# Four double blocks of layer one in teams, with pieces of plain items between the first team periods

## The chip, the cores and the metric

The kernel runs on one core of one Trainium2 chip. The metric is the time of one execution in microseconds on the device, as a median of several runs. TensorE does the matmuls, VectorE (DVE), ScalarE (ACT) and GpSimd (POOL) the elementwise work, and SyncE (SP) issues most of the transfers.

## What is computed

An attention over channels (256 x 256 scores over 6016 tokens) gives x, and two gated layers follow, each from 256 to 1536 and back to 256 features:

```
x1 = rmsnorm(x) * rms_g
y  = (silu(x1 @ w_gate) * (x1 @ w_val)) @ w_out          # layer one
z  = (sigmoid(y @ w2_gate) * (y @ w2_val)) @ w2_out      # layer two
```

## The kernel before

Every float32 operand is split into a high and a low part of the type that TensorE reads fast, and each product is three matmuls (`mm3`: high x high, high x low, low x high). The 6016 tokens are 47 tiles of 128, in 12 blocks of four tiles (block 5 has three). Two blocks are a pair, also called a double block; there are six, and pair 2, with block 5, is 448 columns wide per half, the others 512. The hidden features are 12 tiles, f = 0 to 11.

Layer one's first two pairs (blocks 0 to 3) are worked **plain**: an item is one block and one f. It has 12 matmuls for gate and value (`plain_gv`, into PSUM banks `g` and `v`) and 6 for the output, issued two items later (`SKEW`). Behind them ScalarE takes the gate, VectorE the product (L478), ScalarE the high part `hh` (L479) and VectorE the low part `hl` (L480). While the 48 plain items run, the weights of both layers are converted from 64-bit inputs in five groups of steps for each of 24 weight tiles (`conversion`, `ORDER`). `quota` says how many groups each item takes along, so that all are done five items ahead of the stage's end (`end`), and each tile of layer one before block 0 needs it (`ahead` lists which of the blocks 0 and 1 comes next).

All later pairs use a Strassen-like scheme with seven input products instead of eight (`product`: 11, S1, T2, 12, T3, S4, P4). One f of a pair is a **period**. Z, A and B are its PSUM accumulators. ScalarE copies Z to A (cpA), to `g1` (cpG) and to the bank for the fourth product (cpD), and B to `e5`; VectorE forms `v1` and `g1`; in the next period (`pv`) the gate is applied (gate, h1, h0) and the fourth product P4 is made.

Pair 2 of layer one is worked **alone** (`period`): it reads the plain stage's weights `wh`, `wl` in SBUF, and its output products are plain, four a period. All pairs after it are worked in **teams** (`joint`, `team_period`): six periods' hidden tiles `hs` are combined by a second seven-product scheme for the output, whose 21 products (`out_product`) run in the six periods that follow. Team periods read their split weights from DRAM (`gw_load` from `gd`, two periods ahead, three buffers) and combined output weights from `od` (`ow_load`). The six first team periods have no team before them to finish. Their order is the list NONE; later ones use EVEN and ODD.

Output weights reach `od` in halves: raw ones are read back (`out_load`), split (`out_high` on ScalarE, `out_low` on VectorE, which then stores), then combined on GpSimd (`out_sums`) and split again. Layer one's twelve halves and six of layer two's stand in the alone stage, the other six in layer one's later team periods. The alone stage also stores the gate and value weights into `gd` (`store_w`). The next pair is loaded and summed on GpSimd (`pair_load`, `pair_sums`) and split (`pair_high`, `pair_low`) during the current one. The order on every engine is that of the program; each engine works through its queue in order.

## Time and profile before

| | us |
|---|---|
| median of 3 runs | 1170.33 (1166.58 to 1170.48) |
| profiled execution | 1170.04 |
| its span, first to last instruction | 1168.3 |
| mean granted TensorE clock | 0.996 of full speed |

The attention takes the first 105 us; plain items follow to about 305, the alone stage to about 392, the first six team periods to about 424, and layer two's pairs begin near 660. In the rows below a line such as L480 is a line of the kernel before; PE is TensorE's matmuls, PEld its weight loads, and "x284" counts instructions that touch the stretch.

### The profile page before, as it was taken

The page shows a single profiled execution, that of the slowest core. Times are in us where ns is not written, and L with a number is a line of the kernel's source. Part 1 is how long each engine was busy: PE and PEld are TensorE (multiplying, and loading weights), DVE is VectorE, ACT ScalarE, POOL GpSimd, SP SyncE. Part 2 cuts the span into 40 slices and gives each one's busy share as a digit, 9 for nine tenths or more (in the row PEclk, how much of TensorE's full clock was granted, in tenths as well). Part 3 has the DMA queues.
Part 4 walks back from the last instruction along what each step waited for, and adds up shares of the span by engine and source line. Part 5 has one row for each costly group of instructions (what it writes and reads, how often), then busy time and mean ns, then how long its engine had stood idle before and what let it go on. Part 6 is the DMA issues. An engine that isn't in the chain of part 4 may idle for free.

```text
span 1168.3 us, 16678 instructions
## 1 busy us (share of the span) xinstructions
PE 1148.7 (98%) x5236; PEld 957.0 (82%) x5236; DVE 968.3 (83%) x1496; ACT 890.2 (76%) x1664; POOL 334.3 (29%) x398
## 2 busy tenths in 40 slices
PE   8899999999999999999999999999999999999998
PEld 7788788888898778888888788888888888888896
DVE  6798999886667688888888887888888888888877
ACT  6666788775577687887787887787787787787685
POOL 0043677454223322321321321311311321321121
PEclk9899999999999999999999999999999999999999
DMA  9663445867489989999999998998998998998995
GB/s 329 241 220 143 145 148 190 282 228 238 145 280 322 355 258 266 303 264 266 303 262 272 300 258 251 287 265 245 288 265 240 293 260 247 293 261 245 284 273 147
DMA packets 142856, 296.84 MB, mean 254 GB/s; under 512 B 13872, under 2 KB 53168, under 8 KB 142768
## 3 DMA queue, kind: packets, MB, share of 16 engines
q1 hardware_dynamic: 122032, 258.65, 65.6%
q0 software_dynamic: 20592, 37.00, 18.1%
q8 instruction: 41, 0.67, 0.2%
q14 instruction: 47, 0.39, 0.1%
q10 hardware_dynamic: 144, 0.13, 0.0%
HBM read 201.98 MB, written 56.75 MB: 221 GB/s over the span
## 4 chain that ended last, share of the span: by engine, by line
PE 84%; DVE 8%; DMA 4%; issue 2%; ACT 2%; POOL 1%; SPq 0%; DVEq 0%; POOLq 0%; ACTq 0%
PE g L107 12%; PE g L109 12%; PE g L108 12%; PE v L107 6%; PE v L108 6%; PE v L109 6%; PE y L108 5%; PE y L109 5%; PE y L107 5%; PE at L108 4%; PE at L107 4%; PE at L109 4%; DMA in<-in_q_dram 1%; PE y L973 1%; DVE xn L329 1%
## 5 line engine op out<-in xcount | busy, mean ns | idle before, releaser
L605 POOL DMA_DIRECT2D hs<-hs x143 | 124.7, 918 | 571.5 <-DVE hl L688 413.6
L688 DVE TENSOR_TENSOR hl<-hs,hh 128x512 fp32r<-128x512 f32 (+1 forms) x319 | 221.1, 704 | 25.1 <-ACT hh L657 24.2
L657 ACT CAST hh<-hs 128x512 fp32r<-128x512 f32 (+1 forms) x319 | 192.6, 615 | 25.7 <-PE at L109 6.5
L874 ACT COPY v<-g 128x512 f32<-128x512 f32 (+1 forms) x210 | 119.0, 567 | 63.1 <-PE g L109 59.8
L879 DVE TENSOR_TENSOR hs<-g,e 128x512 f32<-128x512 f32 (+1 forms) x105 | 71.5, 681 | 66.5 <-ACT v L874 65.6
L107 PE MATMUL g<-xh,gw 128*128 128x512 f32 x240 | 94.1, 392 | 0.7 <-DVE hs L879 0.6
L108 PE MATMUL g<-xl,gw 128*128 128x512 f32 x240 | 93.5, 389 | 0.0
L109 PE MATMUL g<-xh,gw 128*128 128x512 f32 x240 | 93.4, 389 | 0.0
L908 ACT ACTIVATE g<-g 128x512 f32<-128x512 f32 (+1 forms) x108 | 67.5, 625 | 30.4 <-DVE g L912 29.4
L107 PE MATMUL y<-hh,ow 128*128 128x512 f32 (+1 forms) x211 | 81.7, 387 | 0.2 <-issue 0.2
L108 PE MATMUL y<-hl,ow 128*128 128x512 f32 (+1 forms) x211 | 81.7, 387 | 0.0
L109 PE MATMUL y<-hh,ow 128*128 128x512 f32 (+1 forms) x211 | 81.6, 387 | 0.0
L874 ACT COPY g<-g 128x512 f32<-128x512 f32 (+1 forms) x105 | 61.3, 583 | 26.2 <-PE g L109 25.8
L912 DVE TENSOR_TENSOR g<-g,g 128x512 f32<-128x512 f32 (+1 forms) x105 | 70.3, 669 | 5.7 <-PE g L109 5.7
L883 ACT ACTIVATE sg<-v 128x512 f32<-128x512 f32 (+1 forms) x108 | 64.2, 594 | 7.5
L107 PE MATMUL g<-qh,gw 128*128 128x512 f32 (+1 forms) x171 | 66.5, 389 | 0.7 <-DVE hs L879 0.6
L109 PE MATMUL g<-qh,gw 128*128 128x512 f32 (+1 forms) x171 | 65.8, 385 | 0.0
L108 PE MATMUL g<-ql,gw 128*128 128x512 f32 (+1 forms) x171 | 65.8, 385 | 0.0
L108 PE MATMUL at<-hl,ow 128*128 128x512 f32 (+1 forms) x160 | 62.4, 390 | 0.6 <-DVE hl L688 0.6
L107 PE MATMUL at<-hh,ow 128*128 128x512 f32 (+1 forms) x160 | 62.2, 389 | 0.3 <-ACT hh L657 0.2
L109 PE MATMUL at<-hh,ow 128*128 128x512 f32 (+1 forms) x160 | 61.9, 387 | 0.0
L874 ACT COPY e<-g 128x512 f32<-128x512 f32 (+1 forms) x105 | 61.3, 584 | 0.4
(256 smaller groups left out, 3312.4 us busy)
## 6 DMA issues: line engine op xcount, KB each, us to landing
gw<-gd SPq DMA_DIRECT2D x216, 448.0 KB, 5.6
ow<-od SPq DMA_DIRECT2D x126, 384.0 KB, 5.4
hs<-hs POOLq DMA_DIRECT2D x128, 256.0 KB, 7.7
wraw<-in_w_dram SPq DMA_DIRECT2D x24, 768.0 KB, 5.3
od<-o SPq DMA_DIRECT2D x48, 256.0 KB, 4.6
vraw<-in_v_t_dram SPq DMA_DIRECT2D x11, 512.0 KB, 4.9
gd<-w2h SPq DMA_DIRECT2D x12, 448.0 KB, 2.6
gd<-w2l SPq DMA_DIRECT2D x12, 448.0 KB, 3.6
```

The lines of the kernel that those rows point to most:

```text
L107: nc.tensor.matmul(ps, sh, mh, start=start, stop=False, skip_group_check=more)
L108: nc.tensor.matmul(ps, sh, ml, start=False, stop=False, skip_group_check=more)
L109: nc.tensor.matmul(ps, sl, mh, start=False, stop=stop, skip_group_check=more)
L329: nc.vector.tensor_scalar_mul(xn[b][:, i], ps[i // 2][:, i % 2], rs[:, i : i + 1])
L605: nc.gpsimd.dma_start(out=to, in_=t, accum_op=ALU.add)
L657: nc.scalar.copy(h, src)
L688: nc.vector.tensor_sub(lo, src, f32(h))
L874: nc.scalar.copy(new(name, make, *args), s[src])
L879: nc.vector.tensor_add(s["v1"], s["Z"], s["e5"])
L883: nc.scalar.activation(out=new("sg0", lambda: t), in_=s["A"], func=acts[l])
L908: "gate": lambda: nc.scalar.activation(out=pv["g1"], in_=pv["g1"], func=acts[pl]),
L912: "g1": lambda: nc.vector.tensor_add(s["g1"], s["g1"], s["B"]),
```

## The change

- Pair 2 of layer one joins the teams, as layer one's last pair. `period` and `parts`, which worked it alone, are gone (not shown).
- The plain stage stops three items early (`LATE`). The pieces of these items (gate and value matmuls singly, output matmuls) go through the queue `plain` and take the two places "out" of the six first team periods. NONE has a new order, and Z and B of these periods stand in the single banks `y1` and `y0`.
- Layer one's split weights are stored to `gd` during the plain stage (`stored`, `store_plain`). The output weights in plain form go to `od` straight from `wh`, `wl` (`store_out`), so that of layer one only the combined halves are split, at hooks in the plain stage. Layer two's twelve halves are all split in the first six team periods (`soon_halves`).
- `ahead` puts block 0's items 8 and 9 one place later, and conversions must end at item 40 instead of 43.

```diff
...
+    LATE = 3
...
+    NW = NQ - A11
...
         def high():
             if l:
-                h = cv2.tile([P, NG, P], F32R, tag="w2h", name="w2h")
+                h = w["sh"] = cv2.tile([P, NG, P], F32R, tag="w2h", name="w2h")
+                nc.scalar.copy(h[:, A11:], w["t"][:, A11:NG])
             else:
-                h = wp.tile([P, NQ, P], F32R, tag=f"wh{f}", name="wh")
-            own = slice(A11, NG if l else NQ)
-            nc.scalar.copy(h[:, own], w["t"][:, own])
-            w["h"] = wh[l, f] = h
+                h = wh[l, f] = wp.tile([P, NW, P], F32R, tag=f"wh{f}", name="wh")
+                nc.scalar.copy(h, w["t"][:, A11:])
+            w["h"] = h
...
         def sums_high():
-            h = w["h"]
+            if not l:
+                w["sh"] = cv2.tile([P, NG, P], F32R, tag="w2h", name="w2h")
+            h = w["sh"]
             nc.scalar.copy(h[:, :A11], w["t"][:, :A11])
-            if l:
-                w["3h"] = h[:, S3 : S3 + 1]
-            else:
-                w["3h"] = cv1.tile([P, 1, P], F32R, tag="s3h", name="s3h")
-            nc.scalar.copy(w["3h"], w["s3"])
+            nc.scalar.copy(h[:, S3 : S3 + 1], w["s3"])
...
         def stored():
-            if l:
-                nc.sync.dma_start(out=gd[l][f][:, 0], in_=f32(w["h"]))
-                nc.sync.dma_start(out=gd[l][f][:, 1], in_=f32(w["l"]))
-                del wh[l, f], wl[l, f]
-            else:
-                nc.sync.dma_start(out=s3d[f][:, 0], in_=f32(w["3h"])[:, 0])
-                nc.sync.dma_start(out=s3d[f][:, 1], in_=f32(w["3l"])[:, 0])
+            for e, t in enumerate((w["sh"], w["sl"])):
+                if l:
+                    nc.sync.dma_start(out=gd[l][f][:, e], in_=f32(t))
+                else:
+                    nc.sync.dma_start(out=gd[l][f][:, e, :A11], in_=f32(t[:, :A11]))
+                    nc.sync.dma_start(out=gd[l][f][:, e, S3], in_=f32(t[:, S3]))
...
     ORDER = (
-        "-high units shifted", "-low", "whole signed", "size -s_high -s_low rounded", "guarded sums -stored"
+        "-high units shifted",
+        "-low",
+        "whole signed",
+        "size -s_high rounded -s_low -stored",
+        "guarded sums",
...
-    def plain_gv(it):
+    def plain_one(it, m, late=False):
         b, f = it
         w = sizes[b] * P
-        gv[it] = [gv_bank("g"), gv_bank("v")]
-        for m, ps in enumerate(gv[it]):
-            for c, (h, lo) in enumerate(xT[b]):
-                j = A11 + 2 * m + c
-                mm3(ps[:, :w], wh[0, f][:, j], wl[0, f][:, j], h[:, :w], lo[:, :w], c == 0, c == KC - 1)
+        ps = gv_bank("gv"[m and not late])
+        gv.setdefault(it, []).append(ps)
+        for c, (h, lo) in enumerate(xT[b]):
+            j = 2 * m + c
+            mm3(ps[:, :w], wh[0, f][:, j], wl[0, f][:, j], h[:, :w], lo[:, :w], c == 0, c == KC - 1)
+
+    def plain_gv(it):
+        plain_one(it, 0)
+        plain_one(it, 1)
...
-    alone = [(0, PLAIN, f) for f in range(NF)]
-    joint = [(0, p, f) for p in range(PLAIN + 1, NP) for f in range(NF)]
+    joint = [(0, p, f) for p in (*range(PLAIN + 1, NP), PLAIN) for f in range(NF)]
     joint += [(1, p, f) for p in (0, 1, 3, 4, 5, 2) for f in range(NF)]
-    stream = alone + joint
...
+    soon_pairs = [(1, i) for i in range(NF // 2)]
...
     def out_load(l, i):
-        if l and i < NJ:
-            w = [wp.tile([P, 2, 512], F32, tag=lent_out[(NJ * i + u) % 4], name="o") for u in range(3)]
-            o = [w[u // 2][:, u % 2] for u in range(5)]
+        if l == 0:
+            odd[l, i] = [cv2.tile([P, 512], F32, tag="ot", name="o")]
         else:
-            if l:
-                o = [ip3.tile([P, 512], F32, tag="yo", name="o") for _ in range(3)]
-            else:
-                o = [wp.tile([P, 512], F32, tag=lent_in[i], name="o") if i in lent_in else sp.tile([P, 512], F32, tag="t1", name="o")]
-                o += [sp.tile([P, 512], F32, tag=f"t{u}", name="o") for u in (2, 3)]
-            o += o[1:]
-        odd[l, i] = {"t": o[0], 0: o[1:3], 4: o[3:]}
-        nc.sync.dma_start(out=o[0], in_=rd[l][i].rearrange("p u n -> p (u n)"))
+            odd[l, i] = [sp.tile([P, 512], F32, tag=f"o{u}", name="o") for u in (i % 2, 2, 3)]
+        nc.sync.dma_start(out=odd[l, i][0], in_=rd[l][i].rearrange("p u n -> p (u n)"))
 
     def out_high(l, i, first):
-        nc.scalar.copy(odd[l, i][first][0].bitcast(F32R), odd[l, i]["t"])
+        if l == 0:
+            odd[l, i] += [cv2.tile([P, 512], F32, tag=t, name=t) for t in ("oh", "ol")]
+        elif first:
+            odd[l, i] = [odd[l, i][3]] + [sp.tile([P, 512], F32, tag=f"o{u}", name="o") for u in (4, 5)]
+        nc.scalar.copy(odd[l, i][1].bitcast(F32R), odd[l, i][0])
 
     def out_low(l, i, first):
-        h, lo = odd[l, i][first]
-        nc.vector.tensor_sub(lo.bitcast(F32R), odd[l, i]["t"], h)
+        h, lo = odd[l, i][1:3]
+        nc.vector.tensor_sub(lo.bitcast(F32R), odd[l, i][0], h)
         g, j = divmod(i, NJ)
         for e, t in enumerate((h, lo)):
             dst = od[l][g][:, first : first + 4, e, j]
             nc.sync.dma_start(out=dst, in_=t.rearrange("p (u n) -> p u n", u=4))
 
     def out_sums(l, i):
-        w11, w21, w12, w22 = (odd[l, i]["t"][:, u * P : (u + 1) * P] for u in range(4))
-        nc.gpsimd.tensor_add(w22, w21, w22)
-        nc.gpsimd.tensor_sub(w21, w11, w21)
-        nc.gpsimd.tensor_sub(w11, w22, w11)
-        nc.gpsimd.tensor_sub(w12, w11, w12)
+        o = odd[l, i]
+        if l:
+            o.append(sp.tile([P, 512], F32, tag=f"o{6 + i % 2}", name="o"))
+        w11, w21, w12, w22 = (o[0][:, u * P : (u + 1) * P] for u in range(4))
+        s2, s3, s4, s1 = (o[-1][:, u * P : (u + 1) * P] for u in range(4))
+        nc.gpsimd.tensor_add(s1, w21, w22)
+        nc.gpsimd.tensor_sub(s3, w11, w21)
+        nc.gpsimd.tensor_sub(s2, s1, w11)
+        nc.gpsimd.tensor_sub(s4, s2, w12)
...
     NONE = (
-        "11 S1 cpA gate h1 P4 third part1 T2 e5 12 flush h0 first"
-        " gw early part0 out out cpG ACT out sg T3 cpD out S4 end"
-        " DVE g1 v1"
+        "gate h1 11 gw P4 S1 h0 DVE cpA early T2 12 third e5"
+        " first cpG end T3 sg S4 cpD v1 ACT flush g1 out out"
...
         def out():
-            if outs:
-                outs.popleft()()
-                outs.popleft()()
+            if plain:
+                plain.popleft()()
             else:
                 out_product()
...
-            return (at_bank, j) if n < HALF and n % 2 else (gv_bank, "g")
+            return (y_bank, j) if n < HALF else (gv_bank, "g")
...
-        ahead = [0, 0, 1] + 10 * [0, 1]
+        ahead = [0, 0, 1, 0, 1, 0, 1, 0, 1, 0, 1, 0, 1, 0, 1, 1, 0, 1, 0, 0, 1, 0, 1]
...
+        now = len(items) - LATE
+        end = now - 5
+
+        def store_plain(f):
+            for e, t in enumerate((wh[0, f], wl[0, f])):
+                nc.sync.dma_start(out=gd[0][f][:, e, A11:S3], in_=f32(t[:, : S3 - A11]))
+                nc.sync.dma_start(out=gd[0][f][:, e, A22], in_=f32(t[:, A22 - A11]))
+
+        def store_out(f):
+            g, j = divmod(f // 2, NJ)
+            for e, t in enumerate((wh[0, f], wl[0, f])):
+                nc.sync.dma_start(out=od[0][g][:, f % 2 * 2 : f % 2 * 2 + 2, e, j], in_=f32(t[:, 2 * KC :]))
 
         for f in range(NF):
-            hook(at[2 * PLAIN - 1, f], load_s3, f)
+            hook(at[1, f] + 1, store_plain, f)
+            hook(at[2 * PLAIN - 1, f], store_out, f)
+        for u, n in enumerate([16, 16, 23, 28, 30, 32]):
+            hook(n, out_load, 0, u)
+            hook(n + 2, out_sums, 0, u)
+            hook(n + 3, out_high, 0, u, 4)
+            hook(n + 3, out_low, 0, u, 4)
+        for n in range(3):
+            hook(at[2 * PLAIN - 1, n] + 4, gw_load, n)
...
+        def soon_halves(n):
+            if n < len(soon_pairs):
+                for first in (0, 4):
+                    out_high(*soon_pairs[n], first)
+                    out_low(*soon_pairs[n], first)
+            if n + 2 < len(soon_pairs):
+                out_load(*soon_pairs[n + 2])
+            if n + 1 < len(soon_pairs):
+                out_sums(*soon_pairs[n + 1])
...
+        def plain_out(n):
+            b, f = items[n]
+            for c in range(KC):
+                out_mm(0, b // 2, b % 2, f, c)
+            if f == NF - 1:
+                for c in range(KC):
+                    evacuate(0, b // 2, b % 2, c, c, f32(hidden("hh")))
+
+        def plain_rest(n):
+            plain_one(items[n], 1, True)
+            plain_h(items[n])
+            for fn in hooks.get(n, ()):
+                fn()
+
+        for n in range(now, len(items)):
+            plain.extend((partial(plain_one, items[n], 0), partial(plain_rest, n), partial(plain_out, n - SKEW)))
+        plain.extend(partial(plain_out, n - SKEW) for n in range(len(items), len(items) + SKEW))
...
-        for n, it in enumerate([*stream, None]):
+        for n, it in enumerate([*joint, None]):
...
-            if 0 < n // NF < 4 and f == NF - 3:
-                u = n // NF + 2
-                slots[0].setdefault("end", []).append(partial(out_load, 1, u))
-                slots[1].setdefault("end", []).extend(halves(1, u, 0))
-            if 1 < n // NF < 5 and f == 0:
-                slots[1].setdefault("end", []).extend(halves(1, n // NF + 1, 4))
-            if n == 0:
-                for f in range(NF):
-                    slots[f].setdefault("end", []).append(partial(store_w, f))
...
+            if n < HALF:
+                slots[0].setdefault("end", []).append(partial(soon_halves, n))
...
```

## Rows read from the trace of the kernel before

**Rows 1.** The page, part 1: busy us, share of the span, instructions.

```profile
PE 1148.7 (98%) x5236; PEld 957.0 (82%) x5236; DVE 968.3 (83%) x1496; ACT 890.2 (76%) x1664; POOL 334.3 (29%) x398
```

**Rows 2.** Windows: stretch, us, busy time by engine (instructions), clock, DMA share, GB/s.

```profile
760.00:835.00 75.00, 75.00 (x333) 62.06 (x332) 63.66 (x102) 60.37 (x111) 16.94 (x18) 1.00 0.93 264
1112.00:1125.00 13.00, 13.00 (x66) 12.05 (x65) 10.69 (x20) 11.34 (x25) 4.59 (x6) 1.00 0.99 276
305.00:392.00 87.00, 85.56 (x410) 76.14 (x410) 60.41 (x99) 63.40 (x124) 27.03 (x40) 1.00 0.87 296
392.00:424.00 32.00, 31.80 (x131) 23.74 (x130) 21.13 (x32) 22.43 (x43) 7.15 (x6) 1.00 0.92 310
424.00:745.00 321.00, 319.76 (x1402) 261.87 (x1401) 273.49 (x432) 259.95 (x474) 81.07 (x88) 1.00 0.95 274
745.00:1050.00 305.00, 304.88 (x1343) 251.25 (x1342) 259.05 (x412) 244.60 (x447) 67.94 (x72) 1.00 0.93 266
```

**Rows 3.** Windows of the plain stage, same columns.

```profile
121.00:185.00 64.00, 64.00 (x284) 52.98 (x283) 62.91 (x76) 50.45 (x86) 46.41 (x54) 1.00 0.49 159
...
201.00:249.00 48.00, 48.00 (x211) 39.30 (x210) 42.77 (x57) 35.53 (x63) 25.34 (x36) 1.00 0.76 255
```

**Rows 4.** Waits of PEld, 305 to 430 us: total us, times, longest us.

```profile
PEld at L108 <- DVE hl L769: 2.8, 7, 0.6
...
PEld at L107 <- ACT g L874: 1.3, 3, 0.4
```

**Rows 5.** Waits of PEld, 430 to 745, then 745 to 1130 us.

```profile
PEld g L107 <- DVE hs L879: 2.8, 4, 1.0
...
PEld g L107 <- DVE hs L879: 1.4, 3, 0.5
```

**Rows 6.** Groups by line and form, 392 to 424 us: busy us, mean ns | idle before.

```profile
L912 DVE TENSOR_TENSOR g<-g,g 128x512 f32<-128x512 f32 x3 | 2.1, 687 | 5.7 <-PE g L109 5.7
...
L874 ACT COPY g<-g 128x512 f32<-128x512 f32 x3 | 1.8, 590 | 0.8 <-PE g L109 0.8
```

**Rows 7.** DMA: 300 to 366, 366 to 412, 120 to 200 us; KB, us to landing.

```profile
od<-o SPq DMA_DIRECT2D x21, 256.0 KB, 2.2
...
DMA packets 12959, 16.08 MB, mean 350 GB/s; under 512 B 753, under 2 KB 9457, under 8 KB 12955
...
od<-o SPq DMA_DIRECT2D x16, 256.0 KB, 6.1
...
wraw<-in_w_dram SPq DMA_DIRECT2D x11, 768.0 KB, 4.5
```

**Rows 8.** Timeline near 122 and 175 us: start us, us, engine, line, operation.

```profile
122.48 0.39 PE L109 MATMUL v<-qh,wl 128*128 128x512 f32 x1
...
125.76 0.69 DVE L480 TENSOR_TENSOR hl<-v,hh 128x512 fp32r<-128x512 f32 x1
...
175.52 0.39 PE L109 MATMUL v<-qh,wl 128*128 128x512 f32 x1
...
181.19 0.68 DVE L480 TENSOR_TENSOR hl<-v,hh 128x512 fp32r<-128x512 f32 x1
```

**Rows 9.** Groups by line and form, 305 to 392 us.

```profile
L563 DVE TENSOR_TENSOR o<-o 128x512 fp32r<-128x512 f32 x18 | 11.8, 685 | 0.2 <-DMA od<-o 0.2
...
L571 POOL TENSOR_TENSOR o<-o 128x128 f32<-128x128 f32 x9 | 6.4, 713 | 51.7 <-DVE o L563 31.4 <-PE g L109 20.3
```

**Rows 10.** Groups by line and form, 105 to 305 us.

```profile
L166 DVE SCALAR_TENSOR_TENSOR wst<-wst,wbits 128x768 f32<-128x768 f32 x22 | 27.9, 1270 | 0.3
...
L195 DVE TENSOR_TENSOR wl<-wst,wh 128x768 fp32r<-128x768 f32 x10 | 11.4, 1141 | 0.1
...
L195 DVE TENSOR_TENSOR w2l<-wst,w2h 128x512 fp32r<-128x512 f32 x12 | 8.7, 725 | 0.0
```

**Rows 11.** Timeline near 407 us, VectorE and GpSimd.

```profile
407.63 1.48 DVE L585 SCALAR_TENSOR_TENSOR hs<-hs,g 128x512 f32<-128x512 f32 x1 [0.54 <-ACT g L908]
...
407.26 1.30 POOL L410 TENSOR_TENSOR xs<-xl 128x512 f32<-128x512 f32 x1
```

More of the change, by code (lines that the diff above doesn't have):

```diff
@@ L923, in team_period @@
         for step in (EVEN, ODD)[n % 2] if n >= HALF else NONE:
-            do.get(step, partial(at, step))()
+            if pv or step not in ("gate", "h1", "P4", "h0", "first"):
+                do.get(step, partial(at, step))()
         return s
@@ L1181, in quota, with halves @@
             return most
-        first = stream[0][:2]
-        for n, it in enumerate(items):
+        def halves(l, i, first):
+            steps = [partial(out_high, l, i, first), partial(out_low, l, i, first)]
+            return steps if first else [*steps, partial(out_sums, l, i)]
+        def soon_halves(n):
[7 more added lines that the diff above has]
+                out_sums(*soon_pairs[n + 1])
+        first = joint[0][:2]
+        for n, it in enumerate(items[:now]):
             if n == end:
@@ L1230 @@
                 slots.extend({} for _ in range(NF))
[L1231 to L1237 removed]
+                if n + NF < len(joint):
+                    nxt = joint[n + NF][:2]
                     own = ((n // NF) % 2) == 1
@@ L1281 @@
             pv = s
-            outs = [(*it[:2], e, it[2]) for e in (1, 0)] if n < len(alone) else []
 def kernel(**inputs):
```

152 lines of the change are left out of this document (27 added, 125 removed), and 8 rows, old and new, of tables (EVEN, ODD).

## The prediction

> **What bounds the kernel now.** I read the page first: TensorE is busy 98% of the span [rows 1]. That invites the sentence "count the matmuls", but a busy TensorE need not be at its pace, so the second view is the windows, for the pace; the granted clock is 1.00 of the upper level, 2.4 GHz, in all of them. In an undisturbed stretch of the team stage 75 us hold 333 matmul records, some two of them at the edges: 75/331 = 0.2266 us for one of 512 columns. In a stretch of 448-column work 13 us hold 64, 0.203 us [rows 2]. With these two figures each stage can be asked what it loses. The plain stage loses nothing over long stretches: 64 us with 284 records, 282 inside, is 0.227 [rows 3]. From 305 to 392 us, where pair 2 works alone, there are, by the order of the code, 385 matmuls of 448 columns and 24 of 512 (its neighbours' at both ends): 83.6 us of work, 3.4 lost. From 392 to 424 us, the first six team periods, 123 of 512 and 7 of 448: 29.3 us, 2.7 lost. From 424 to 745 us: 1400 x 0.2266 = 317.3, so 3.7 lost; from 745 to 1050 us, the same code in layer two: 1341 x 0.2266 = 303.9, only 1.1 lost [rows 2]. So what this change can touch is 3.4 + 2.7 + 2.6 us of stalls and the number of matmuls; everything else is TensorE at its pace.
>
> The third view, the waits of the weight loads, says who causes the stalls: alone, the `hl` parts of VectorE come late for the output matmuls; in the first team periods the matmul of T3 waits for ScalarE's copy of Z, some 0.4 us each time, where 0.1 is the engine's own spacing [rows 4]. In layer one's later periods VectorE's sum into `hs` is late four times by 2.8 us in all, against 1.4 us for three times in layer two [rows 5].
>
> **Term 1, the matmuls that go.** A double block outside a team takes 7 input products and 4 output products for each f, each of 3 matmuls: 33. In a team it takes 21 + 63/6 = 31.5. Twelve f save 18 matmuls of 448 columns: 18 x 0.203 = 3.65 us less. The 45 plain items before and the pieces of three later are the same 48 x 18 matmuls. There is no cover here: TensorE sets the pace on both sides, so the term counts in full, and it has no range.
>
> **Term 2, the stretch that is replaced.** It lost 3.4 + 2.7 = 6.1 us. What stands there now is six periods of 21 input matmuls with 12 of plain pieces: 33 x 0.2266 = 7.48 us each, which is pure pace. I follow the new order NONE through one period. 11, P4, S1 take 2.04 us; T2 needs cpA, a copy of 0.6 like all of ScalarE's here [rows 6], which can start at 0.9: in time. Then only product 12 (0.68 us) stands between T2 and T3, and T3 overwrites Z, which cpG is still reading. It is the order that the old kernel has in its first team periods, and there the wait is 0.27 us over pace [rows 4]. Six of those: 1.6 us. In the first period there is no P4, so T2 waits likewise, 0.3. S4 and the two pieces cover 2.72 us behind it, in which cpD, v1 and g1 (0.6, and 0.69 for each of VectorE's two [rows 6]) are done, so that one `y` bank each for Z and B suffices. ScalarE has 3.5 us of its own six steps, 1.2 for two split copies, 0.6 for a pair copy and on average 0.6 for the plain gate and copy, 5.9 of 7.5; VectorE about 5.8.
>
> Where a period *ends* with `plain_rest` (the first and the fourth), ScalarE's copy `hi` stands behind VectorE's product, which needs the matmul that ended the period; gate and cpA are queued behind it on ScalarE. Counted from the next period's start: product 0.2 to 0.9, `hi` to 1.5, gate to 2.1, cpA to 2.7, while T2 wants to start at 2.04: 0.75 us late, twice, 1.5. In the third period `plain_rest` comes first and is hidden. With 0.3 for the pair sums of the next double block and 0.3 at the start of the first team, the stretch loses 4.0 us: 2.1 us gained. Ends: 1.9 (only T3 and T2) and 9 (every period late by its 1.5 us chain). I take the sum since each piece has a row.
>
> The transfers of these periods: each period stores 1 MB of split weights, reads 0.25 MB of raw ones and 0.9 MB of `gw`: 2.2 MB in 7.8 us is 280 GB/s, with 1 MB more in the first and 0.8 MB more in the fourth and fifth. Before, 16 MB went in 46 us (350 GB/s) and split stores took 6.1 us to land, against 2.2 us in the stretch before it [rows 7]. A period's split copies need the last period's stores landed, about 4 us after the last of them is issued. Between 280 and 350 I take 0 and keep 3 us as the end.
>
> **Term 3, the splits that leave the later team periods.** Six half splits, their sums on GpSimd and their stores stood in layer one's periods; now they are all in the first six. The 45 periods up to 745 us lost 3.7; at layer two's rate (1.1 us in 42.7 periods) they and the 12 new team periods of pair 2 lose 57 x 0.026 = 1.5. Gain 2.2 us. Ends: 0, if the stalls come from something else, and 2.6.
>
> **Term 4, the plain stage pays.** This is the cost side, and here VectorE is the engine to look at: 62.9 of 64 us busy from 121 to 185 us while it is at three steps of weight conversion in an item, then 42.8 of 48 at two and a half [rows 3]. What it lets slip shows in the distance from an item's last `v` matmul (start plus 0.39) to the end of its `hl`: 3.6 us in item 3 (122.87 to 126.45), 6.0 us in item 16 (175.91 to 181.87) [rows 8], 0.18 us more with each item. TensorE doesn't feel it until the same `v` bank is wanted again two items later, 6.6 us after that matmul (8.16 for two items of 18 matmuls, less the 1.5 that the six `v` matmuls themselves take). The change ends the conversions at item 40, not 43: the formula of `quota` gives three steps through item 30 instead of 15. Also six half splits of layer one (0.69 us each on VectorE) and six times four sums on GpSimd, of at most 0.71 us each [rows 9], come in, two of both at items 18 and 19. Item by item: 6.0 at item 16, 6.4 at 18 (two more of 0.18), then 1.4 for two splits and 0.5 for GpSimd in the way (priced below): 8.3, so 1.7 over the limit. Then layer two's conversions, lighter by 1.14 - 0.73 us each on the line that splits them, though L166 at 1.27 us stays [rows 10], hold the distance level to item 30; one more split with its sums adds 0.9 there. 2.6 us lost. SyncE gets four more stores an item and four where two small ones were, ahead of the raw weights that land 4.5 us after issue [rows 7] and are wanted six steps (8.2 us) later: 0.6 more, an estimate between 0 and the 2 us that four issues and their bytes could take. 3.2 us. Ends: 0, since at two and a half steps VectorE still had 5 of 48 us idle [rows 3], so that the whole work may fit, and 9, if the 0.18 goes on through item 30 (2.5), all six splits count (4.1) and GpSimd costs 0.4 each time.
>
> GpSimd's price: beside a GpSimd instruction of 1.30 us a VectorE product with both inputs in SBUF took 1.48 us, where its like take 0.69 [rows 6, 11]: 0.8 lost. So I take 0.4 to 0.5 for each call of sums of 0.71 that meets such an operation. The Trainium skill, page "SBUF — State Buffer", section "Who interferes with whom", says that VectorE instructions with two SBUF inputs and GpSimd instructions that read SBUF exclude each other for a whole instruction. This row agrees; by that rule alone all 24 moved sums could each hold VectorE up for their length, 17 us at most, instead of the 0.9 that the sum has for them.
>
> **Sum.** -3.65 - 2.1 - 2.2 + 3.2 = -4.75 us. The profiled execution took 1170.04 us (span 1168.3), close to the median of 1170.33: 1165.3 us, 0.4% less.
>
> **Rivals.**
> - *The plain stage hides it* (VectorE has a tenth of its time idle from 201 us on [rows 3], and TensorE has not yet reached the bank limit): -8 us, 1162. Against it: the two splits at item 19 meet the largest distance of the stage.
> - *The plain stage gives all back*: 8 us there, 1170. For it: the 98% of [rows 3].
> - *The new periods are as bad as the old ones*: single `y` banks and the blocked ScalarE queue cost 8 instead of 4, or the stores are late by 3: 1169 to 1170.
> - *Slower*: GpSimd's 24 sums hold VectorE up each time. 24 x 0.71 = 17.0 [rows 9], and 4.1 for the splits: 21.1 lost in the plain stage, net +13.2, 1183. It turns the sign from 7.95 us lost there (3.65 + 2.1 + 2.2). Against it: in [rows 3] GpSimd is busy 46.4 of 64 us and TensorE still loses nothing.
>
> **Chances.** Forecast (1163 to 1168) 0.5; hidden 0.18; all given back 0.13; bad periods 0.12; slower 0.07. 0.5% is 5.9 us, about what a measurement of this kernel can tell from no change (the three runs span 3.9 us). Faster by more than that means below 1164.5: all of the hidden case and 0.2 of the forecast's lower side, 0.38. Slower by more: the last rival, 0.06. The rest 0.56. Eight in ten: from 1161, just below the hidden case, to 1171.5, which takes in the two cases at 1170 with something over.
>
> **What would show it.** The profile after should hold 18 matmuls fewer; a pace of 0.227 us up to about 180 us and 1 to 4 us lost from 180 to 235, with weight loads that wait for VectorE; six waits of T3 for the copy of Z in `y` banks and two longer ones of T2; no `o` instructions in later team periods, and layer one's loss per period down to layer two's. The prediction is wrong if plain items run at 4.08 us throughout, if split copies wait for `od` stores, or if the later layer-one periods lose as much as before.

## The result, and the profile after

Before 1169.64 us (median of 4 runs, 1166.58 to 1170.48), after 1181.88 us (median of 4, 1180.05 to 1184.69): ratio 1.0112, 95% interval 1.0084 to 1.0139. The change makes the kernel 1.1% slower; the forecast was 1165.3. The profiled execution after has a span of 1180.4 us, 12.1 more than the 1168.3 of before.

The page, part 1, of the changed kernel:

```profile
PE 1149.1 (97%) x5218; PEld 952.8 (81%) x5218; DVE 982.9 (83%) x1524; ACT 894.9 (76%) x1678; POOL 353.4 (30%) x414
```

18 matmuls fewer than in [rows 1], as the change says, and hardly any difference in busy time: the 12 us are idle time of TensorE. The windows of the changed kernel (columns as in [rows 2]) say where:

```profile
121.00:185.00 64.00, 63.93 (x281) 52.73 (x282) 61.12 (x76) 49.20 (x83) 45.52 (x54) 1.00 0.78 243
180.00:284.00 104.00, 94.86 (x400) 73.53 (x399) 93.69 (x121) 75.53 (x135) 76.36 (x102) 1.00 0.93 306
201.00:249.00 48.00, 42.79 (x178) 32.75 (x179) 42.83 (x58) 35.89 (x64) 30.36 (x42) 1.00 0.95 319
305.80:360.00 54.20, 50.05 (x205) 37.20 (x204) 37.85 (x54) 34.29 (x65) 17.48 (x22) 1.00 0.96 282
360.00:451.70 91.70, 91.40 (x399) 74.12 (x398) 77.69 (x125) 73.27 (x136) 21.68 (x23) 1.00 0.93 271
...
760.00:835.00 75.00, 74.96 (x331) 61.73 (x330) 64.70 (x104) 60.74 (x111) 12.62 (x14) 1.00 0.91 256
```

The pace is what it was (75 us hold 331), and up to 185 us the plain stage loses next to nothing (281 where [rows 3] has 284). From 201 to 249 us TensorE starts 178 matmuls where [rows 3] has 211, and VectorE is busy 42.83 us in place of 42.77: it does as much work and gets less far with the items, so its busy share alone does not show the trouble. For the whole disturbed part of the plain stage take 180 to 284 us; the kernel before has there:

```profile
180.00:284.00 104.00, 104.00 (x457) 85.60 (x457) 92.03 (x122) 77.52 (x135) 56.50 (x80) 1.00 0.69 235
```

Loss in a window is its length less 0.2267 us for each matmul: 104 - 457 x 0.2267 = 0.4 before, 104 - 400 x 0.2267 = 13.3 after. This window measures every experiment below. How far one execution can be trusted is shown by two kernels further down whose plain stage is the same as the changed kernel's (half splits spread; stores left out): they have 400 and 403 matmuls there, 13.3 and 12.6 us lost. The first six team periods, 305.8 to 360 us, lose 54.2 - 205 x 0.2267 = 7.7 us (7.9 from the distances of successive matmul starts less their pace, the measure used where no window is shown); the stretch that they replace lost 6.1. Layer one's team periods behind them lose 4.1 us by that measure, 3.6 before. The first plain matmul starts at 105.6 us, 0.8 later. Over the whole plain stage that measure gives 13.1 us more than before. Together, attention, plain stage, stretch, later periods and the matmuls that went: 0.8 + 13.1 + 1.6 + 0.5 - 3.65 = 12.35, against 12.1 measured.

What the engines wait for after the change: total us, times, longest; the first four lines from 121 to 290 us, the next three (weight loads) and the last two from 305 to 362. The line numbers are the changed kernel's: its L481, L482 and L483 are the product, `hh` and `hl`, L557 and L561 the split copies and differences of output weights, L573 to L576 their sums, L149 the first step on raw weights.

```profile
PEld v L108 <- DVE hl L483: 13.1, 14, 1.8
...
DVE wbits L149 <- DMA wraw<-in_w_dram: 6.5, 7, 1.8
DVE ol L561 <- ACT oh L557: 3.3, 3, 2.1
ACT oh L557 <- POOL o L576: 3.3, 2, 2.5
...
PEld y L108 <- ACT v L813: 4.1, 4, 1.4
PEld y L108 <- ACT g L813: 2.5, 6, 0.4
PEld g L108 <- ACT v L813: 1.9, 1, 1.9
...
ACT o L557 <- DMA od<-o: 2.0, 2, 1.1
...
DVE o L561 <- DMA od<-o: 2.7, 2, 2.0
```

Fourteen times the `v` bank is not free because VectorE's `hl` of two items before is not done: the limit that the prediction named. The timeline of the changed kernel (start us, us, engine, line, operation, [idle before <- releaser]), where it is first reached and where it hurts most:

```profile
176.28 0.39 PE L110 MATMUL v<-qh,wl 128*128 128x512 f32 x1
...
182.65 0.68 DVE L483 TENSOR_TENSOR hl<-v,hh 128x512 fp32r<-128x512 f32 x1
...
183.38 0.19 PEld L108 LDWEIGHTS v<-qh,wh 128*128 128x128 f32 x1 [0.33 <-DVE hl L483]
...
191.60 0.58 DVE L149 TENSOR_SCALAR wbits<-wraw 128x768 uint32<-128x768 uint32 x1 [1.79 <-DMA wraw<-in_w_dram]
...
192.10 0.68 DVE L483 TENSOR_TENSOR hl<-v,hh 128x512 fp32r<-128x512 f32 x1
...
192.83 0.19 PEld L108 LDWEIGHTS v<-qh,wh 128*128 128x128 f32 x1 [1.42 <-DVE hl L483]
...
199.41 0.47 POOL L576 TENSOR_TENSOR o<-o 128x128 f32<-128x128 f32 x1
...
199.91 0.62 ACT L557 CAST oh<-o 128x512 fp32r<-128x512 f32 x1 [2.47 <-POOL o L576]
...
200.56 0.82 DVE L561 TENSOR_TENSOR ol<-o,oh 128x512 fp32r<-128x512 f32 x1 [2.08 <-ACT oh L557]
...
201.07 0.19 PEld L108 LDWEIGHTS g<-qh,wh 128*128 128x128 f32 x1 [1.53 <-ACT sg L480]
```

The last `v` matmul of item 16 ends at 176.67, its `hl` at 183.33: 6.66 us (in [rows 8] that distance was 6.0), and the weight load that needs the bank, for item 18, starts 0.05 us behind it after a wait of 0.33. At 191.6 VectorE had stood 1.79 us for a raw weight, and the next `v` waits 1.42. At 199.9 ScalarE had stood 2.47 us at the head of its queue for GpSimd's last sum; the gate behind it, VectorE's difference and TensorE's next `g` stand too. Three suspects lie in these ten lines: late raw weights, GpSimd's sums, and VectorE with no time left.

### The profile page after: what moved, and what is told of

Read it like the earlier page. It is cut to its first block, busy times and chain, and to the rows that moved or that the text cites. A ratio compares the mean times of both kernels' runs of the same rounds, so it can differ in the third digit from the quotient of the medians.

```text
span 1180.4 us, 16825 instructions
## 1 busy us (share of the span) xinstructions
PE 1149.1 (97%) x5218; PEld 952.8 (81%) x5218; DVE 982.9 (83%) x1524; ACT 894.9 (76%) x1678; POOL 353.4 (30%) x414
## 4 chain that ended last, share of the span: by engine, by line
PE 77%; DVE 8%; DMA 6%; issue 4%; ACT 2%; POOL 2%; SPq 0%; DVEq 0%; POOLq 0%; ACTq 0%
PE g L108 12%; PE g L110 11%; PE g L109 11%; PE v L108 5%; PE y L108 5%; PE v L109 5%; PE v L110 5%; PE y L109 5%; PE y L110 5%; PE at L109 4%; PE at L110 4%; PE at L108 4%; DMA in<-in_q_dram 2%; DMA wraw<-in_w_dram 2%; DVE xn L328 1%
## 5 line engine op out<-in xcount | busy, mean ns | idle before, releaser
L607 POOL DMA_DIRECT2D hs<-hs x159 | 138.7, 922 | 638.1 <-DVE hl L690 485.4
L690 DVE TENSOR_TENSOR hl<-hs,hh 128x512 fp32r<-128x512 f32 (+1 forms) x355 | 242.4, 694 | 28.3 <-ACT hh L659 26.5
L659 ACT CAST hh<-hs 128x512 fp32r<-128x512 f32 (+1 forms) x355 | 212.8, 610 | 31.0 <-PE at L110 9.6
L813 ACT COPY v<-g 128x512 f32<-128x512 f32 (+1 forms) x228 | 128.1, 562 | 66.1 <-PE g L110 62.9
L108 PE MATMUL g<-xh,gw 128*128 128x512 f32 x270 | 106.0, 392 | 1.5 <-ACT v L813 1.5
L109 PE MATMUL g<-xl,gw 128*128 128x512 f32 x270 | 105.2, 390 | 0.0
L110 PE MATMUL g<-xh,gw 128*128 128x512 f32 x270 | 105.2, 390 | 0.0
L108 PE MATMUL y<-hh,ow 128*128 128x512 f32 (+1 forms) x235 | 90.6, 385 | 0.2 <-issue 0.2
L109 PE MATMUL y<-hl,ow 128*128 128x512 f32 (+1 forms) x235 | 90.6, 385 | 0.0
L110 PE MATMUL y<-hh,ow 128*128 128x512 f32 (+1 forms) x235 | 90.5, 385 | 0.0
L813 ACT COPY g<-g 128x512 f32<-128x512 f32 (+1 forms) x114 | 65.9, 578 | 29.5 <-PE g L110 29.4
L109 PE MATMUL at<-hl,ow 128*128 128x512 f32 (+1 forms) x178 | 69.1, 388 | 0.8 <-DVE hl L690 0.8
L108 PE MATMUL at<-hh,ow 128*128 128x512 f32 (+1 forms) x178 | 68.9, 387 | 0.3 <-ACT hh L659 0.2
L110 PE MATMUL at<-hh,ow 128*128 128x512 f32 (+1 forms) x178 | 68.5, 385 | 0.0
L813 ACT COPY e<-g 128x512 f32<-128x512 f32 (+1 forms) x114 | 66.1, 580 | 0.5
```

Of the source, the lines that this page charges most:

```text
L108: nc.tensor.matmul(ps, sh, mh, start=start, stop=False, skip_group_check=more)
L109: nc.tensor.matmul(ps, sh, ml, start=False, stop=False, skip_group_check=more)
L110: nc.tensor.matmul(ps, sl, mh, start=False, stop=stop, skip_group_check=more)
L607: nc.gpsimd.dma_start(out=to, in_=t, accum_op=ALU.add)
L659: nc.scalar.copy(h, src)
L690: nc.vector.tensor_sub(lo, src, f32(h))
```

## The experiments

The attention in front of the plain stage took 100.9 to 106.0 us from run to run, in which nothing was changed; so single executions are compared by stage, and a median or a ratio stands where there are several. Where the granted clock in a window fell, its loss holds the extra time of matmuls at the lower level, 1.2 GHz; the text says how much, from the distances of matmul starts.

**Raw weights earlier.** Theory A: SyncE's longer list of stores makes the raw weights late. The load is issued one group of steps earlier.

```diff
+                    if name == "-stored" and i + 2 < len(conversions):
+                        run.append(partial(load_w, *conversions[i + 2]))
...
-            if i + 2 < len(conversions):
-                steps[-1].append(partial(load_w, *conversions[i + 2]))
```

> One edit: the load of the raw weights of a later conversion is issued on SyncE's queue ahead of the stores of the split sums, no longer behind them. The changed kernel loses 13.5 us over pace between 185 and 281 us, the kernel before 0.6 in the same stretch. Theory A (raw weights come late, since their load stands behind stores that wait for GpSimd): the loss falls to 5 us or less, raw weights land 1.5 us or more before use, time about 1173. Theory B (VectorE simply has too much work at three groups of steps an item): 10 us or more stay, time 1179 or more.

1181.05 us; the window:

```profile
180.00:284.00 104.00, 95.74 (x407) 75.13 (x406) 95.09 (x122) 75.70 (x135) 78.40 (x103) 1.00 0.92 305
```

VectorE's wait for raw weights is gone (6.5 to 0 us), but 11.7 us are lost in place of 13.3. Late weights cost 1.6 us, not 13, and theory A falls; VectorE's waits for ScalarE's split copies grew from 3.3 to 5.3 us in their place.

**No combined output weights.** Their reading, sums, copies, differences and stores left out (plain weights are stored in their place, so the output is not the reference's).

```diff
...
-            hook(n, out_load, 0, u)
-            hook(n + 2, out_sums, 0, u)
-            hook(n + 3, out_high, 0, u, 4)
-            hook(n + 3, out_low, 0, u, 4)
+            pass
```

> Left out: reading back, combining and splitting layer one's combined output weights in the plain stage (six loads, 24 GpSimd sums, six splits); plain weights are stored in their place, so layer one's output is another one. Theory A: GpSimd's queue is 20 us shorter and so SyncE waits less for it; the loss of 13.5 us falls to 5 to 8, with loads still late now and then. Theory B: it falls only by what VectorE is spared, 4 to 5 us, to about 9. Theory C (GpSimd holds VectorE up through the shared SBUF access): VectorE's operations with two SBUF inputs get shorter by more than 5 us in all.

1178.3 us; the window:

```profile
180.00:284.00 104.00, 101.10 (x435) 80.64 (x435) 88.41 (x118) 74.61 (x132) 57.80 (x79) 1.00 0.88 293
```

5.4 us lost: 7.9 of the 13.3 belong to the six combined splits. The rest stays without them. The loss is where theory A put it, but not by its way: VectorE still waits 5.4 us for raw weights (the last line of the first fence on VectorE's groups below).

**All 48 plain items ahead of the teams.**

```diff
-    LATE = 3
+    LATE = 0
```

> LATE is 0: all 48 plain items run in the plain stage, conversions end at item 43 as before, no pieces are left for the first team periods but the last two output products. Theory B: with two and a half groups an item again, the loss between 185 and 281 us falls below 4. Theory A: the order on SyncE's queue is the same, so 8 us or more stay. Either way the six first team periods have 21 matmuls each, run at VectorE's and ScalarE's pace and lose 10 us or more against the time of their matmuls, so the time is about 1180.

1182.88 us; the window:

```profile
180.00:284.00 104.00, 99.97 (x428) 81.04 (x428) 92.61 (x122) 76.21 (x133) 69.38 (x98) 0.98 0.91 304
```

7.0 us lost, between the two theories: with three more items for the conversions 6.3 us come back. Some 1.5 of the 7.0 are extra time of matmuls at the lower clock. But without pieces among the first team periods the stretch up to the first team output loses 18.1 us (2.9 of them at the lower clock) in place of 7.9. The pieces pay for the room that they take.

**Both of the first two.**

> Both edits, the raw load first and no combined splits (plain weights stored in their place, so layer one's output is another one). Theory A: 3 us or less of the 13.5 stay in the plain stage, time about 1171. Theory B: 8 us or more stay.

1178.42 us; the window:

```profile
180.00:284.00 104.00, 101.21 (x439) 81.36 (x438) 90.86 (x120) 74.94 (x133) 60.67 (x80) 1.00 0.88 287
```

4.5 us lost, again between the theories. No split, next to no late weight, and still 4.5: three steps of conversion an item leave VectorE no room for what else stands there in both kernels. The trace shows which part of it comes first. The distance from the last `v` matmul to the end of `hl` is 5.6 to 5.9 us from item 15 to item 21, level at three steps; at item 22, where VectorE waits 1.3 us for ScalarE's `qh` and works 1.3 us on two `ql` (the `q` splits of the second pair), it is 7.7, over the limit of 6.6 for the first time, and TensorE stands.

What the plain stage gains without these splits is in part lost in the stretch behind it. There the kernel without combined weights loses 13.8 us and the one with both edits 12.4, where the changed kernel loses 7.9; 3.1 and 1.7 of that come from the lower clock, and ScalarE's split copies wait 6.0 and 6.3 us for `od` stores in place of 2.0. Both kernels store plain weights twice late in the plain stage; a kernel below that does not, the one without the sums, loses 9.2 there. Whether those stores, or the stretch's earlier start, make the others late was not tested. So the window says what a piece of work costs in its stage, and not what the kernel would gain without it.

**The plain differences on GpSimd; the splits staggered.** Theory D: the differences only wait at the wrong place in VectorE's queue. Both kernels have the earlier raw weights.

```diff
-        nc.vector.tensor_sub(lo.bitcast(F32R), odd[l, i][0], h)
+        (nc.vector if l else nc.gpsimd).tensor_sub(lo.bitcast(F32R), odd[l, i][0], h)
```

> Raw load first, and the low parts of layer one's six combined output weights are formed on GpSimd, no longer on VectorE. With the raw load first alone the plain stage lost 12.2 us over pace, and VectorE fell 4.4 us further behind in the one item with two splits. Theory D (a split costs little by its own 0.69 us; VectorE stands in its queue until GpSimd's sums and ScalarE's copy of them are done): the loss falls to about 5, what it is without any split. Theory B alone (only VectorE's own work counts): it falls by 6 times 0.69, to about 8. If GpSimd's extra operations hold VectorE up instead, it stays above 10.

```diff
-        for u, n in enumerate([16, 16, 23, 28, 30, 32]):
+        for u, n in enumerate([18, 21, 24, 27, 30, 33]):
...
-            hook(n + 3, out_low, 0, u, 4)
+            hook(n + 4, out_low, 0, u, 4)
```

> Raw load first, and the six splits stand apart (sums at items 20, 23, 26, 29, 32, 35, ScalarE's copy one item later, VectorE's subtraction one item after that). VectorE has the same work, but what it needs has been done an item before. Theory D: the loss in the plain stage falls from 12.2 to about 8 or 9, the 5 that stay without splits and 4 for six subtractions. If the splits' own work is the cost, it stays above 11.

1188.67 and 1183.63 us; the windows:

```profile
180.00:284.00 104.00, 94.94 (x394) 73.42 (x393) 93.61 (x112) 73.36 (x131) 82.38 (x106) 0.98 0.89 290
```

```profile
180.00:284.00 104.00, 95.92 (x397) 75.22 (x396) 91.44 (x118) 73.78 (x132) 76.23 (x99) 0.97 0.88 293
```

14.7 and 14.0 us lost, where the kernel that they start from loses 11.7. The lower clock makes some 1.5 of the first and 2.6 of the second, so the first is worse and the second level; neither gains. The waits of the first, 121 to 305 us:

```profile
ACT oh L557 <- POOL o L576: 6.2, 5, 1.6
...
DVE v L481 <- ACT sg L480: 4.0, 4, 2.0
```

GpSimd's sums come later, ScalarE's copy holds its queue longer for them (2.9 us in the kernel that they start from), and VectorE waits for gates. In the staggered kernel the same two lines have 8.3 and 6.7 us. Neither kernel comes near the 5 or the 8 to 9 us of theory D, which falls as far as these two edits can show it: the waits moved, they did not go. GpSimd's sums come under suspicion.

**The sums alone, the splits alone.** First the 24 sums left out, then the six copies and differences (in both, plain weights are stored in place of combined ones; the output is not the reference's).

```diff
...
-            hook(n + 2, out_sums, 0, u)
```

> The changed kernel with the 24 sums of the combined output weights of layer one left out: the six readings, copies, differences and stores stay, so plain weights are stored in place of combined ones. GpSimd theory (the sums are late on a busy GpSimd, and the copies of ScalarE wait for them at the head of its queue): the plain stage falls from 13.7 us lost to 6 to 8, near the 5.8 of the run without any of it. VectorE theory (VectorE has no room for six more differences, whoever makes their inputs): 11 to 13 stay. Half of each: about 10.

```diff
...
-            hook(n + 3, out_high, 0, u, 4)
-            hook(n + 3, out_low, 0, u, 4)
```

> The other half alone: readings and the 24 sums on GpSimd stay, the six copies and differences are left out, and plain weights are stored in place of combined ones, as in the run without any of it. Nothing waits for the sums any more. If GpSimd's sums cost by holding VectorE's operations with two inputs in SBUF, the plain stage keeps 9 us or more; if only by what waits for them, or not at all, it falls to 5 to 7.

1179.27 and 1177.31 us. The window without the sums:

```profile
180.00:284.00 104.00, 97.74 (x415) 76.63 (x414) 93.05 (x124) 77.60 (x138) 59.45 (x81) 1.00 0.96 319
```

and without the splits:

```profile
180.00:284.00 104.00, 97.74 (x418) 77.36 (x417) 88.22 (x115) 73.23 (x130) 74.61 (x101) 1.00 0.88 296
```

9.9 and 9.2 us lost. So: neither 5.4, splits alone 9.9, sums alone 9.2, both 13.3 (the readings stand in the last three). The two add up within the spread of single executions: splits cost 4.5 or 4.1, sums 3.8 or 3.4, whichever is taken out first. Neither theory was right alone. How can sums that nobody waits for cost 3.8? VectorE's groups from 160 to 290 us without either (busy us, mean ns | idle before):

```profile
L159 DVE SCALAR_TENSOR_TENSOR wbits<-wraw,wbits 128x768 uint32<-128x768 uint32 x15 | 15.7, 1046 | 0.0
L167 DVE SCALAR_TENSOR_TENSOR wst<-wst,wbits 128x768 f32<-128x768 f32 x15 | 15.7, 1044 | 0.4
L164 DVE CUSTOM_DVE_ANT_0 wbits<-wbits,wunits 128x1536 uint16<-128x1536 uint16 x15 | 14.4, 958 | 1.0
L149 DVE TENSOR_SCALAR wbits<-wraw 128x768 uint32<-128x768 uint32 x14 | 10.3, 736 | 5.5 <-DMA wraw<-in_w_dram 5.4
```

and with the sums alone:

```profile
L159 DVE SCALAR_TENSOR_TENSOR wbits<-wraw,wbits 128x768 uint32<-128x768 uint32 x15 | 16.6, 1107 | 0.0
L167 DVE SCALAR_TENSOR_TENSOR wst<-wst,wbits 128x768 f32<-128x768 f32 x15 | 16.1, 1071 | 0.4
L164 DVE CUSTOM_DVE_ANT_0 wbits<-wbits,wunits 128x1536 uint16<-128x1536 uint16 x15 | 14.7, 981 | 1.0
L149 DVE TENSOR_SCALAR wbits<-wraw 128x768 uint32<-128x768 uint32 x14 | 11.1, 793 | 7.2 <-DMA wraw<-in_w_dram 7.2
```

The same instructions take 0.9 + 0.4 + 0.3 + 0.8 = 2.4 us longer, and VectorE waits 1.8 us more for raw weights (that the readings make them late is argued, not shown): 4.2 us of VectorE's time, for which TensorE pays 3.8. The longer times do come from GpSimd: the instructions of L159 that run beside none of GpSimd's take 0.95 us on average in both kernels (seven and one of them) and in the kernel before; with the sums alone the five that run beside a sum take 1.12. That is the price of GpSimd beside VectorE: 2.4 us for 24 sums, where the forecast had 0.5 at item 19 and part of 0.9 later. By the rule of the Trainium skill, page "SBUF — State Buffer", section "Who interferes with whom", it could have been 17 by the prediction's estimate. The direction agrees (three of the four lines have two inputs in SBUF; L149 is a `tensor_scalar`, which the section lists among those that can contend); the size is a seventh.

**Layer two's half splits, one to a period.** Over twelve team periods in place of two in each of six.

```diff
...
-            if n < HALF:
-                slots[0].setdefault("end", []).append(partial(soon_halves, n))
+            if n < NF:
+                slots[0].setdefault("end", []).append(partial(soon_half, n))
```

> Layer two's twelve half splits run one in each of the first twelve team periods, no longer two in each of the first six; the plain stage is that of the changed kernel. Theory E (in the first periods ScalarE stands until the last period's split weights have landed in DRAM, with the transfers near their limit): the loss over pace from the stage's start to the end of the seventh period falls from 9.3 to 6 us, the waits of split copies for od stores vanish, and the waits of T2 and T3 stay. If the periods lose by their chain of copies alone, it stays at 8 to 9. The next six periods lose 0 to 1 us more.

1178.82 us; the two windows up to the first team output and behind it:

```profile
302.70:353.40 50.70, 48.98 (x206) 37.61 (x205) 31.11 (x48) 31.85 (x59) 10.99 (x14) 1.00 0.85 260
353.40:447.90 94.50, 92.53 (x397) 73.49 (x396) 81.58 (x129) 75.73 (x140) 26.44 (x31) 1.00 0.98 286
```

50.7 - 46.7 = 4.0 us, where the changed kernel has 7.7. (It is the number that was forecast for this stretch, but with one half split to a period, not two.) But the next 400 matmuls lose 94.5 - 90.0 = 4.5, against 91.7 - 399 x 0.2267 = 1.2, and not 0 to 1 more. Most of the gain is paid back later.

**All three edits.** Earlier raw weights, differences on GpSimd and spread half splits together.

> Raw load first, low parts on GpSimd and halves spread over twelve periods. If theories D and E hold, the two gains add up: about 8.5 us less in the plain stage and 3 less in the first periods than in the changed kernel, 1170.

1186.61 us, not 1170; 396 matmuls in the window, 14.2 lost, and 7.8 in the stretch, 1.5 of them at the lower clock. GpSimd's share spoils the plain stage.

**Layer two's stores left out** of the first six periods (one split is stored in their place later; the output is not the reference's).

```diff
-            nc.sync.dma_start(out=dst, in_=t.rearrange("p (u n) -> p u n", u=4))
+            if l == 0:
+                nc.sync.dma_start(out=dst, in_=t.rearrange("p (u n) -> p u n", u=4))
...
```

> The changed kernel with the 24 stores of layer two's split output weights left out of the first six team periods (stores of one split stand in for them in periods 12 to 35, so that something is there to read; the output is not the reference's). Stores theory (the split copies of ScalarE and VectorE wait for stores that are late to land): the stretch up to the first team output falls from 7.9 us lost to 4 to 5, as when the splits were spread. Engines theory (the twelve splits themselves, 1.2 us on ScalarE and 1.4 us on VectorE in each period, make the gates and copies late): 7 to 8 stay. Plain stage as in the changed kernel, 13 to 14.

1177.46 us; the stretch, and the waits of weight loads in it (L814 is the changed kernel's L813):

```profile
303.90:356.10 52.20, 49.67 (x206) 37.43 (x205) 37.49 (x54) 34.25 (x65) 15.63 (x22) 1.00 0.65 197
```

```profile
PEld y L108 <- ACT v L814: 4.0, 4, 1.3
PEld y L108 <- ACT g L814: 2.5, 6, 0.4
```

52.2 - 46.7 = 5.5 us: between the theories. What went is the one wait of 1.9 us for a `g` bank at the end of the six periods; the four waits of T2 and six of T3 stand as they were, to a tenth. So the stores cost 2 us, and the other 1.5 over the forecast stand without them: the copies of T2 and T3 come late by the engines' own work. Whether a second set of buffers for the split copies would hide the stores was not tried.

**Everything found to cost, moved.** Raw weights earlier, layer one's six combined splits in the first six team periods, layer two's half splits one to a period behind them; then the same with the pieces of one plain item among the periods (`LATE = 1`); then with two (`LATE = 2`) and layer two's half splits in every second period.

```diff
...
+        soon = [(0, i, 4) for i in range(NF // 2)]
+        soon += [(1, i, first) for i in range(NF // 2) for first in (0, 4)]
...
-            if n < HALF:
-                slots[0].setdefault("end", []).append(partial(soon_halves, n))
+            if n < len(soon):
+                slots[0].setdefault("end", []).append(partial(soon_half, n))
```

> Everything that was found to cost, put elsewhere: raw weights read a step group earlier, the six combined splits of layer one in the first six team periods, layer two's twelve half splits one to a period behind them. By the runs so far the plain stage keeps what its density alone costs, 5 to 6 us, the stretch up to the first team output is near the 4.4 us of the run with spread splits, and the later periods lose some 4 us instead of 1.6: 13.7 - 5.5 = 8.2 and 7.9 - 4.4 = 3.5 less, 2.5 to 3 more, so some 9 us less than the changed kernel, 1172 to 1174, still not below the kernel before. If the plain stage is as long without these splits (their place was not the cause), 1177 or more.

> The same, with the pieces of one plain item instead of three among the team periods, so that the weight conversions have 42 items instead of 40. Density theory: the plain stage gets back about two thirds of the 5 to 6 us that 40 items cost, and the first team period with nothing to fill it pays back some of it: 1169 to 1172. If the pieces are worth more as filling than the room in the plain stage is: 1174 or more.

> As with the moved splits (six of layer one in the first six team periods, raw weights read earlier), but layer two's twelve half splits stand one to every second period (periods 6 to 28), and the pieces are of two plain items. If a split in every period is what made the later periods lose 9.4 us in the kernel with the moved splits, they lose 5 to 6 here, the plain stage 3 to 4, the stretch about 4 to 6: some 1170, level with the kernel before. If the loss goes with the number of splits wherever they stand, the later periods lose 8 to 9 and the time stays at 1173 to 1174.

Medians 1173.73 (ratio to before 1.0039, interval 1.0023 to 1.0056), 1173.73 (1.0031, 1.0019 to 1.0042) and 1176.18 us (1.0070, 1.0044 to 1.0096). The first gives back two thirds of the loss, none beats the kernel before. The second and the third are slower than was expected of them (1169 to 1172, and 1170 or 1173 to 1174). The first kernel's windows:

```profile
180.00:284.00 104.00, 101.64 (x441) 81.84 (x440) 90.74 (x120) 75.00 (x133) 61.62 (x81) 1.00 0.88 285
294.20:344.50 50.30, 48.99 (x206) 37.62 (x205) 30.93 (x47) 31.86 (x59) 18.56 (x26) 1.00 0.86 265
344.50:444.00 99.50, 95.56 (x399) 73.09 (x398) 85.57 (x135) 78.36 (x146) 35.73 (x43) 1.00 1.03 313
```

and the second's:

```profile
180.00:284.00 104.00, 104.00 (x458) 85.59 (x457) 90.74 (x120) 75.93 (x134) 56.62 (x77) 1.00 0.86 285
299.50:347.00 47.50, 42.70 (x170) 31.88 (x168) 29.84 (x45) 31.07 (x58) 16.64 (x27) 0.96 0.78 247
347.00:444.00 97.00, 94.26 (x399) 73.28 (x398) 85.93 (x136) 78.20 (x146) 35.18 (x43) 1.00 1.06 326
```

Lost in the plain window, the stretch and the 400 matmuls behind it: 4.0, 3.6 and 9.0 us; 0.2, 9.0 and 6.5. Two more items for the conversions bring the plain window back to pace (458 matmuls, as before; the third kernel, with one more item, has 448, 2.4 us lost), and the 36 fewer piece matmuls cost 5.4 in the stretch, 1.5 of it by the lower clock (0.96 in the row). So the loss that stays in the plain window without splits goes with the items that the conversions have: 4.0, 2.4 and 0.2 for 40, 41 and 42. In the third kernel the 400 matmuls lose 5.7 us, but the periods behind them 4 us more than in the first (4.3 in the next 400 matmuls, against 0.1): the half splits cost no less when they stand further apart. Why the second kernel loses 2.5 us less behind the stretch than the first, with the same splits, is open.

## Why the prediction was wrong

- *Term 1, the matmuls: right.* 18 fewer, pace unchanged.
- *Term 4, the plain stage: the step that failed.* Forecast 3.2 us, measured 13.1, over its upper end of 9. The mechanism and the place were right: the `hl` distance passes 6.6 us between items 16 and 18, and weight loads wait for VectorE. The size was not. The working let the two splits at item 19 and their sums cross the limit, one more split later, and added only 0.6 for raw weights. Between them the distance was held level, and without splits it is (5.6 to 5.9 us at three steps); but then VectorE has next to nothing over, and what else comes in is paid: the `q` splits of the second pair, which the working did not have, the later splits, and each call of sums. By the experiments: three steps an item with what stands beside them in both kernels 4.5, late raw weights 0.9 (1.6 with the splits in), sums 3.8, six splits 4.1: 13.3. TensorE does not pay all of VectorE's extra time: 3.8 of 4.2 us for the sums, and 4.1 of 8.3 for the splits (six differences of 0.83 us, and 3.3 us of waits for ScalarE). The upper end of 9 had 2.5 for the density, where 4.5 was measured, nothing for late raw weights, 4.1 for the splits, as measured, and 2.4 for the sums, where 3.8 was measured. Its price of a sum was taken from sums of 0.71 us at most; those in the plain stage took up to 1.2 us.
- *The slower rival* put the loss on GpSimd's 24 sums, 17 us of it; its time, 1183, is close by luck, and its cause is not the right one: sums are 3.8 of 13.3, the plain stage lost 13.1 and not 21.1, and terms 2 and 3, which that sum counts as gained, gave nothing.
- *Term 2, the stretch: mechanism right, size wrong.* Six waits of T3 for the copy of Z, as forecast. Of T2's waits there were four of 1 us on average, not two of 0.75 and a short one; and the stores, taken as 0 between 280 and 350 GB/s with 3 us as the end, cost 2. They landed 4.9 us after issue (24 of them, 256 KB each, 305 to 362 us) against 2.2 in the same place of [rows 7], and that split copies wait for them is one of the signs by which the prediction called itself wrong. 7.9 lost, forecast 4.0. (S4 and two pieces are 15 matmuls, 3.4 us, not 2.72; nothing hangs on it.)
- *Term 3, later periods: wrong.* From 402 to 550 us layer one's periods lost 0.3 us, so the splits gone from them do help as forecast. But 1.3 is lost in the first 42 us behind the stretch and 2.1 around the changes into and out of pair 2 (550 to 600 and 640 to 680 us), which the working gave the rate of layer two; what part of that stood at pair 2's ends before was not taken apart. 4.1 in all, forecast 1.5.
- *Not in the sum:* 0.8 us in the attention, within what it varies from run to run.

That the loss in the plain stage is VectorE's time is shown by the additions and subtractions above, each a single execution; which part of the 4.5 us of density belongs to the `q` splits of the second pair and which to the conversions was not taken apart by an experiment. The trace shows only that the limit is first passed at those splits, and the kernels with 41 and 42 items that fewer conversions an item take the loss away with the `q` splits in place.

## What to carry to other kernels

When an engine off the critical path has no idle time left, price every microsecond that is added to it, its longer operations and waits at its queue's head too (here half to nine tenths of it were paid), and count the work that stands there already; a limit that the forecast reaches at one place was reached at most places behind it. A mean busy share hides this: the distance to the next use of a bank shows it. Work taken out of one stage was not saved here: the splits cost 3 to 8 us wherever they stood, and plain items were worth about as much as filling among team periods as they were as room for conversions. Before moving work, ask which stage has idle time on every engine that the work touches, and on the queues behind them.

## What the runs showed of the hardware

TensorE's granted clock fell after short stalls in some runs and not in others. In the kernel with earlier raw weights TensorE stood 1.3 of 2 us, the clock fell, and then 8 matmuls in 2.5 us ran at the lower level, 1.2 GHz:

```profile
355.00:357.00 2.00, 0.67 (x2) 0.58 (x3) 1.87 (x4) 1.84 (x4) 0.00 (x0) 0.80 1.00 367
357.00:359.50 2.50, 2.50 (x8) 1.91 (x7) 2.04 (x4) 1.41 (x3) 1.04 (x2) 0.50 1.14 347
```

The changed kernel stood 1.45 us at the same place and went on at the upper level, 2.4 GHz:

```profile
357.00:358.50 1.50, 0.05 (x1) 0.00 (x0) 1.40 (x3) 1.18 (x4) 0.00 (x0) 1.00 0.94 325
358.50:362.00 3.50, 3.45 (x15) 2.75 (x16) 3.16 (x6) 3.11 (x6) 1.31 (x2) 1.00 1.11 353
```

One thing differs ahead of them: the kernel with earlier raw weights had stood 0.93 us for the `v` bank just before, up to 353.9 us, and the changed one had not. Such a drop adds some 8 x 0.2 = 1.6 us to the stall before it, the longer ones 2.6; up to 3.1 us of the stretch in a single run were this (in the kernel without combined output weights).
